# Packed keys of six batches: from two PE transpose steps to one PE step and one crossbar transfer

## The chip, the cores and the metric

The kernel runs on one core of one Trainium2 chip. The metric is the device time of one execution in microseconds (us); the profile gives a slightly shorter span, from the first to the last instruction. The core has five engines that run side by side: PE (matmul), DVE (VectorE), ACT (ScalarE), POOL (GpSimd) and SP (here only an issuer of transfers). In the views PEld is PE's loading of weights, and a q behind an engine's name marks an issue of a transfer. A *crossbar transfer* is a DMA that transposes on its way (`dma_start_transpose`). An execution is called slow when it takes over 1.5% more than the fastest of the same kernel.

## The reference, cut to what matters

```python
# batch 8, heads 8, seq 576, head_dim 64, n_pack 32; p is (8, 8, 32, 64)
p_packed = sm_attn(p, k, v)            # p attends to k, v: 32 rows a head
out      = sm_attn(q, p_packed, p_packed)
x = out.transpose(0, 2, 1, 3).reshape(B * S, H * D)
h = x @ w_in                           # 512 -> 2048
g = h * np.cos(h)
result = g @ w_out                     # 2048 -> 512
```

The rows of `p` are the "packed keys" of the title. Their scores against `k` need `p` with the head dimension on the partitions, so `p` has to be transposed once per batch. It is a small job: 8 x 32 rows of 64 per batch.

## The kernel before

For each batch a *slot* of 16 column blocks runs on PE: each block is an h step (four matmuls, L256, called h0 to h15 below), most of them followed by one to three output matmuls (L309) of the batch before as filling. PSUM is divided into `psA`, three buffers of two banks, and `ot`, two of one bank. Every h step, every transpose step in this slot, every pp and every score takes the next `psA` buffer in turn.

```python
A = ctx.enter_context(tc.tile_pool(name="psA", bufs=3, space=PSUM))
O = ctx.enter_context(tc.tile_pool(name="psO", bufs=2, space=PSUM))
...
def xbar(n, b):                         # q or k of batch b through the crossbar
    t = xT[n, b] = att_pool.tile(...)
    nc.sync.dma_start_transpose(out=t, in_=bf[n, b].rearrange("p h x -> p (h x)"))
...
def pack_p(b0, b1, flat=None):          # keys of batches b0..b1-1 on PE
    ng = 2 * (b1 - b0)
    if flat is None:
        flat = psa(BF16).rearrange("p a x -> p (a x)")     # one psA buffer
    for g in range(ng):
        nc.tensor.transpose(flat[:, g * 128:(g + 1) * 128],
                            p_bf[:, 2 * b0 + g].rearrange("p t d -> p (t d)"), ident)
    V.tensor_copy(out=P2[:, b0:b1]..., in_=flat[:, 0:ng * 128])
...
def h_mm(b, fc):
    ps = psa()
    ...                                 # four matmuls into ps
    ACT.activation(out=csv, in_=ps..., func=AF.Sin, bias=PI_HALF)
    def rest():
        V.tensor_tensor(out=gT[b][:, fc, :]..., in0=ps..., in1=csv, op=ALU.mult)
        ...
    return rest
...
slot(1, [..., (7, tk("k", 2, 2)), (9, lambda: pack_p(2, 5)),      # after h9
         (11, lambda: pack_p(5, B)), (12, next_loads)], 4, {3: 3})  # after h11
...                                     # s1(2), pp(2), s2(2), s1(3) ...
xbar("q", 3)
a1_xbar(3)                              # softmax weights of batch 3, crossbar
recips(3)
xbar("k", 4)
...
slot(2, [(7, lambda: pp(3, engs=(ACT, ACT))), (11, lambda: pw2(3))], 5, {11: 3})
```

`pp(b)` multiplies the softmax weights of a batch (a1T) with its permuted v, and so needs both. The loads of v, q and k of the next batches are held on POOL until the transpose of an earlier k has landed.

The softmax here doesn't subtract the row's maximum and nothing guards it: scores larger than these inputs give would overflow.

## Time and profile before

| | before |
|---|---|
| time, median (runs) | 249.25 us (3); 249.08, 249.09, 249.07 and 248.85 in the later comparisons (6, 11, 12, 11) |
| profiled span | 247.0 us |
| PE / DVE / ACT / POOL busy | 95 / 67 / 68 / 23% |
| PE time for the 12 transposes in slot 1 | 0.34 + 0.33 us |
| PE lost in waits of h10 and h13 there | 0.22 + 0.22 us |

The lines behind this table stand in the prediction. The one thing to bring along: with PE at 95% nothing counts that does not free PE or keep it from a wait.

### The profile page before, as it was taken

The numbers are of one execution on the slowest core, as the hardware profiler recorded it, in microseconds if no ns is written. First come the engines' busy times: TensorE is split into PE (matmuls) and PEld (weight loads), VectorE is DVE, ScalarE is ACT, GpSimd is POOL, SyncE is SP. The second block draws the span as 40 slices with busy tenths as digits, with TensorE's granted clock in tenths as the row PEclk, the third lists the DMA queues.
The fourth block names the chain that finished last, engine by engine and source line by source line (L and its number), as shares of the span: only waits on it lengthen the run. The fifth ranks groups of instructions, "written<-read, shape, count | busy, mean of one in ns | idle before, by whom it ended". The sixth has DMA issues, their size and how long they took to land.

```text
span 247.0 us, 5038 instructions
## 1 busy us (share of the span) xinstructions
PE 234.0 (95%) x2004; PEld 131.4 (53%) x2037; DVE 165.9 (67%) x249; ACT 169.0 (68%) x282; POOL 57.7 (23%) x70
## 2 busy tenths in 40 slices
PE   8888799999999999999999999999999999999993
PEld 3454374566545654565446554565456554665452
DVE  3549987678668876678767766678766684886110
ACT  2369799877666887888787776888778684873000
POOL 8342543240500455022404005030500000000000
PEclk9999999999999999999999999999999999999999
DMA  6999999999899999999998986999591113111133
GB/s 86 203 203 206 205 206 229 200 241 165 165 193 167 223 157 217 215 204 161 213 178 170 192 175 83 195 163 184 109 155 26 45 42 85 45 30 55 48 82 85
DMA packets 63175, 37.09 MB, mean 150 GB/s; under 512 B 35792, under 2 KB 58576, under 8 KB 63152
## 3 DMA queue, kind: packets, MB, share of 16 engines
q0 software_dynamic: 23152, 18.75, 49.8%
q1 hardware_dynamic: 39568, 17.83, 34.7%
q10 hardware_dynamic: 432, 0.20, 0.4%
q8 instruction: 16, 0.26, 0.4%
q14 instruction: 7, 0.06, 0.1%
HBM read 37.22 MB, written 9.44 MB: 189 GB/s over the span
## 4 chain that ended last, share of the span: by engine, by line
PE 80%; DMA 10%; DVE 3%; issue 2%; ACT 2%; POOL 2%; DVEq 0%; POOLq 0%
PE ot L309 46%; PE psA L256 22%; DMA vbf<-in_v_dram 10%; PE psA L207 3%; PE psA L129 2%; DVE gT L263 2%; PE psA L183 2%; ACT cosT L260 2%; PE ot L295 1%; PE psA L233 1%; POOL vp L77 1%; ACT ppT L75 1%; POOL kbf L84 1%; PE ot L104 0%; DVE vp L77 0%
## 5 line engine op out<-in xcount | busy, mean ns | idle before, releaser
L309 PE MATMUL ot<-w_out_bf,gT 128*128 128x512 bf16 x481 | 127.0, 379 | 2.2 <-issue 1.4
L263 DVE TENSOR_TENSOR gT<-psA,cosT 128x576 bf16<-128x576 f32 x128 | 93.9, 755 | 28.3 <-ACT cosT L260 27.5
L260 ACT ACTIVATE cosT<-psA 128x576 bf16<-128x576 f32 x128 | 82.4, 652 | 25.1 <-PE psA L256 22.4
L256 PE MATMUL psA<-a2n,PPW 128*128 128x288 bf16 x512 | 83.8, 286 | 1.5 <-DVE PPW L77 0.4
L309 PEld LDWEIGHTS <-gT 128*128 128x128 bf16 x512 | 47.8, 98 | 43.3 <-issue 6.5
L256 PEld LDWEIGHTS <-PPW 128*128 128x128 bf16 x512 | 49.3, 98 | 34.8 <-issue 4.1
L77 DVE CAST PPW<-psA 128x1024 bf16<-128x1024 f32 (+1 forms) x23 | 26.9, 1175 | 11.6 <-PE psA L207 11.5
L267 POOL COPY joint<-gT 128x512 bf16<-128x512 bf16 x16 | 9.8, 615 | 86.1 <-DVE gT L263 86.1
L77 DVE COPY osb<-ot 128x512 f32<-128x512 f32 (+1 forms) x22 | 14.9, 678 | 17.5 <-PE ot L309 7.6
L77 POOL COPY vp<-vbf 96x3072 bf16<-96x3072 bf16 x7 | 19.3, 2751 | 6.5 <-DMA vbf<-in_v_dram 6.5
L75 ACT COPY osb<-ot 128x512 f32<-128x512 f32 (+1 forms) x15 | 8.5, 567 | 15.3 <-PE ot L309 10.6
L243 DVE SCALAR_TENSOR_TENSOR a2n<-a2u,r,lns 128x576 bf16<-128x576 bf16 x16 | 12.3, 812 | 7.3 <-ACT lns L241 7.3
L235 ACT ACTIVATE lns<-psA 128x576 f32<-128x576 f32 x16 | 10.2, 651 | 7.1 <-PE psA L233 6.5
L140 ACT ACTIVATE a<-psA 128x576 bf16<-128x576 f32 x16 | 10.3, 647 | 6.7 <-PE psA L129 6.7
L309 PE MATMUL ot<-w_out_bf,joint 128*128 128x512 bf16 x48 | 13.0, 379 | 0.1
L225 ACT ACTIVATE a2u<-psA,rs 128x576 bf16<-128x576 f32 x16 | 11.0, 737 | 1.4 <-PE psA L129 1.3
L75 ACT CAST ppT<-psA 64x128 bf16<-64x128 f32 x24 | 6.2, 260 | 6.6 <-DVE ppT L77 5.9
L207 PE MATMUL psA<-w_in_bf,ppT 64*32 64x512 bf16 x224 | 10.1, 380 | 0.0
L241 ACT ACTIVATE lns<-lns 128x576 f32<-128x576 f32 x16 | 10.0, 676 | 0.0
L347 PE MATMUL ot<-wz 128*128 128x512 bf16 x23 | 8.2, 491 | 1.4 <-DVE wz L358 1.2
L84 POOL DMA_DIRECT2D vbf<-in_v_dram x8 | 6.2, 775 | 6.2 <-DVE vp L77 4.2
L525 POOL COPY gate<-kT 1x1 bf16<-1x1 bf16 x3 | 0.5, 180 | 30.1 <-DMA kT<-kbf 30.1
(73 smaller groups left out, 154.9 us busy)
## 6 DMA issues: line engine op xcount, KB each, us to landing
kbf<-in_k_dram POOLq DMA_DIRECT2D x8, 576.0 KB, 12.2
vbf<-in_v_dram POOLq DMA_DIRECT2D x8, 576.0 KB, 7.3
qbf<-in_q_dram POOLq DMA_DIRECT2D x8, 576.0 KB, 9.7
out_dram<-osb SPq DMA_DIRECT2D x24, 192.0 KB, 2.6
out_dram<-osb SPq DMA_DIRECT2D x22, 128.0 KB, 2.4
w_in_bf<-in_moe_w_in_dram POOLq DMA_DIRECT2D x4, 512.0 KB, 17.4
w_out_bf<-in_moe_w_out_dram POOLq DMA_DIRECT2D x4, 512.0 KB, 21.1
out_dram<-osb SPq DMA_DIRECT2D x26, 64.0 KB, 2.1
```

Of the source, the lines that this page charges most:

```text
L75: ACT.copy(out=out, in_=in_)
L77: eng.tensor_copy(out=out, in_=in_)
L140: ACT.activation(out=a1[b % 2][:, y, :, 0:TP].rearrange("p (e m) x -> p e m x", e=2), in_=ps[y][:, :, 0:HS].rearrange("p e (m x) -> p e m ...
L207: nc.tensor.matmul(ps[y][32 * x:32 * x + 32, :], ppT[b % 2][r, 2 * x + y, :], w_in_bf[r, x, n * 512:(n + 1) * 512], start=True, stop=True)
L225: ACT.activation(out=a2u[b][:, y].rearrange("p (e x) -> p e x", e=2), in_=ps[y][:, :, 0:HS], func=AF.Exp, scale=rs1[b][:, y:y + 1])
L235: ACT.activation(out=lns[b][:, y].rearrange("p (e x) -> p e x", e=2), in_=ps[:, :, 0:HS], func=AF.Ln)
L241: ACT.activation(out=lns[b][:, y], in_=lns[b][:, y], func=AF.Exp, scale=-1.0)
L243: V.scalar_tensor_tensor(out=a2n[b][:, y], in0=a2u[b][:, y], scalar=r1[b][:, y:y + 1], in1=lns[b][:, y], op0=ALU.mult, op1=ALU.mult)
L256: nc.tensor.matmul(ps[:, e, 0:HS], PPW[b][:, y, fc * 128:(fc + 1) * 128], a2n[b][:, y, e * HS:(e + 1) * HS], start=(y == 0), stop=(y == 1))
L260: ACT.activation(out=csv, in_=ps[:, :, 0:HS], func=AF.Sin, bias=PI_HALF)
L263: V.tensor_tensor(out=gT[b][:, fc, :].rearrange("p (e x) -> p e x", e=2), in0=ps[:, :, 0:HS], in1=csv, op=ALU.mult)
L309: nc.tensor.matmul(pss[c], w, w_out_bf[:, fc, :], start=(fc == 0), stop=(fc == NFC - 1))
```

## The change

The intent is to take packed-key transposes off PE. The keys of batches 4 to 7 are not needed for another 40 us, so a crossbar transfer can bring them; those of batches 2 and 3 stay on PE, in one step.

```diff
     slot(1, [..., (5, tk("k", 2, 0)), (6, tk("k", 2, 1)),
-             (7, tk("k", 2, 2)), (9, lambda: pack_p(2, 5)),
-             (11, lambda: pack_p(5, B)), (12, next_loads)], 4, {3: 3})
+             (7, tk("k", 2, 2)), (9, lambda: pack_p(2, 4)), (12, next_loads)], 4, {3: 3})
@@
     xbar("k", 4)
+    nc.sync.dma_start_transpose(
+        out=P2[:, 4:B].rearrange("p b (g h) n -> p (b g) (h n)", g=2),
+        in_=p_bf[:, 8:2 * B].rearrange("p g t d -> p (g t d)"))
     fill(5)
```

## The prediction

> **What bounds the kernel now.** I began with the busy times on the page, because they say which engine a saving must land on, and then the shares of the chain that ended last.
>
> ```profile
> PE 234.0 (95%) x2004; PEld 131.4 (53%) x2037; DVE 165.9 (67%) x249; ACT 169.0 (68%) x282; POOL 57.7 (23%) x70
> ...
> PE 80%; DMA 10%; DVE 3%; issue 2%; ACT 2%; POOL 2%; DVEq 0%; POOLq 0%
> ```
>
> PE is busy for 95% of the 247.0 us span, with the clock at full speed in every slice. It carries 80% of the chain, and the DMA share of that chain (10%) is all before 29 us, the start-up loads. So an operation taken off PE after 29 us is worth its PE time, and a wait on PE is worth its length. Time on DVE or in the DMA queue is worth nothing unless it makes PE wait. Next I read what the key transposes cost, from the instructions on the packed keys.
>
> ```profile
> L117 PE MATMUL psA<-ident,p_bf x14: 219/219/311, 4.2 to 58.5; 128*128 128x128 bf16 x14
> ```
>
> 219 ns is the latency of one, not what it takes from PE, so I looked at PE's own timeline around the two steps that the change touches (start, length, what).
>
> ```profile
> 55.84 0.50 PE L117 MATMUL psA<-ident,p_bf 128*128 128x128 bf16 x6
> 56.18 0.59 PE L309 MATMUL ot<-w_out_bf,gT 128*128 128x512 bf16 x2
> 56.83 0.65 PE L256 MATMUL psA<-a2n,PPW 128*128 128x288 bf16 x4
> 57.31 0.59 PE L309 MATMUL ot<-w_out_bf,gT 128*128 128x512 bf16 x2
> 57.75 0.65 PE L256 MATMUL psA<-a2n,PPW 128*128 128x288 bf16 x4
> 58.24 0.50 PE L117 MATMUL psA<-ident,p_bf 128*128 128x128 bf16 x6
> 58.57 0.59 PE L309 MATMUL ot<-w_out_bf,gT 128*128 128x512 bf16 x2
> 59.01 0.65 PE L256 MATMUL psA<-a2n,PPW 128*128 128x288 bf16 x4
> 59.49 0.38 PE L309 MATMUL ot<-w_out_bf,gT 128*128 128x512 bf16 x1
> 59.93 0.65 PE L256 MATMUL psA<-a2n,PPW 128*128 128x288 bf16 x4
> ```
>
> Starts give the throughput. Six transposes take 56.18 - 55.84 = 0.34 us, the second time 0.33, thus 56 ns each. Four h matmuls (L256) take 0.49 us, and one output matmul (L309) takes 0.43/2 = 0.215. There are two holes. After 56.18 the two output matmuls are through at 56.61 and the next h starts at 56.83 (0.22 lost). After 59.49 the one is through at 59.71 and the next h starts at 59.93 (0.22 lost again). The chain in order of time says what ends both:
>
> ```profile
> 56.02 0.77 DVE gT L263
> 56.79 0.04 issue
> 56.83 0.65 PE psA L256 x4
> ...
> 59.12 0.77 DVE gT L263
> 59.89 0.04 issue
> 59.93 0.65 PE psA L256 x4
> ```
>
> psA has three buffers, given in turn to h of each column block and to each key transpose step. An h buffer is free only when DVE has multiplied by the cosine. With a key step in the turn, h10 needs the buffer of h8, and h13 that of h11: only two h are in flight, and PE catches up.
>
> **What the Trainium skill says.** "TensorE: Matmul & The Clock Gate", Part 4 (PE-mode transpose): the result lands in PSUM and needs a copy out; it gives about 275 to 390 ns for one of 128x128. The need of a copy agrees (line 119 on DVE, 0.55 us for 768 columns); the duration does not, 219 ns here. The same page, "Wait — 56ns, not 53.3ns?", gives 55.6 ns from start to start at full clock with 128 columns; the 56 ns above agrees, and it is the figure that counts. "Perfetto Trace Analysis", Optimization Strategy: a bubble that repeats can mean too few PSUM buffers; the two 0.22 us holes agree. "DMA: Bandwidth & Descriptors", Rules for kernel authors: crossbar transposes from different queues must be serialized, one beside ordinary transfers needs nothing. All of this kernel's are issued by SP, the new one too; the trace before shows them running beside stores and loads.
>
> **The change part by part.** *Removed:* 8 of 12 transposes in this stretch. The instruction order of the changed kernel has four left after h9 and none after h11; the DVE copies of 768 and 768 columns become one of 512; everything else is in the same order. By throughput that is 8 x 56 = 0.45 us of PE. What arrives has to be walked, because of the holes.
>
> First step (after h9): two fewer transposes would have PE ready 0.11 us earlier, but h10 still waits for h8's multiply to end at 56.79. Gain 0, the hole grows from 0.22 to 0.33. The step still takes a buffer.
>
> Second step (after h11): it goes altogether. h12 follows two output matmuls: 58.24 + 0.43 = 58.67 in place of 59.01, a gain of 0.34. Its buffer is then that of the first key copy, free at about 57.40 + 0.42 (DVE copies: 0.29 us for 256 columns, 0.55 for 768). h13 now needs h10's buffer, which is free at 58.20 + 0.76 = 58.96, before PE gets there at 58.67 + 0.49 + 0.22 = 59.38. The 0.22 hole closes, and the gain is 0.55. h14 needs h11's multiply (ends at 59.88) and comes at 59.38 + 0.49 + 0.43 = 60.30; h15 needs h12's (cosine done about 59.99, multiply about 60.77) and comes at 61.22 against 61.77. So 0.34 + 0.22 = about 0.55 us of PE, more than the 0.45 of the transposes because a buffer wait goes with them. The last cosine is earlier too, so the table load and the first exponentials of batch 2 keep pace.
>
> *Added:* one crossbar transfer of 128 x 1024 bf16, 256 KB, on SP behind that of k4. Of SP's timeline:
>
> ```profile
> 78.50 3.16 SPq L156 DMA_TRANSPOSE a1T<-a  x1
> 81.76 3.04 SPq L93 DMA_TRANSPOSE kT<-kbf  x1
> 84.89 12.19 SPq L316 DMA_DIRECT2D out_dram<-osb  x8
> ```
>
> a1T has 12 blocks of 128 columns; its undisturbed issues take 1.44 to 1.59 us and it lands in 4.0. The new one has 8 blocks: by estimate 8/12 x 1.5 = 1.0 us of SP's time, landing about 1.0 + (4.0 - 1.5) = 3.5 us after 84.9, near 88.4. Its first reader, the scores of batch 4, loads weights at 97.99, so it is some 9 us early. It holds the stores back by about 1 us; they feed nothing soon (four output buffers, and the next two copies come at 89.35 and 95.25).
>
> *Carried to the end?* PE then reaches every later point 0.55 us sooner, while some feeders keep DMA time. Batch 3's pp is the closest:
>
> ```profile
> 80.88 2.75 POOL L77 COPY vp<-vbf 96x3072 bf16<-96x3072 bf16 x1 [2.07 <-DMA vbf<-in_v_dram]
> ...
> 84.43 0.93 PEld L183 LDWEIGHTS <-vp 96*128 96x128 bf16 x24
> ```
>
> v is permuted at 83.63, and a1T lands at 78.50 + 5.2 = 83.7 (its slowest landing). PE would ask at 84.43 - 0.55 = 83.88. That passes with 0.2 to 0.3 us to spare. Sum: 249.25 - 0.55 = 248.70 us.
>
> **The rivals.** *A wait at batch 3's pp takes some of it back.* The slack is only 0.2, and 0.2 us of jitter in the loads would cost 0.1 to 0.2 us: 248.8 to 248.9. *The new transfer delays the loads of v4, q4 and k5.* They wait for k4's transpose to land at 86.7, are issued from 87.67, and q4 lands about 98.5, just before its own transpose at 98.64; then comes a1T of batch 4 (102.43 + 4.0 = 106.4), which pp reads at 108.4. The new bytes come behind k4's in the same queue, and the transfer view shows the engines nearly idle from about 88.8 to 90.2 before the loads start. 262 KB at the 288 GB/s that k4's transpose reached is 0.9 us, which fits. A delay would have to exceed 2.0 - 0.55 = 1.4 us to reach PE. If it did, the gain is gone: 249.2 to 250. *The transposes hide anyway.* Were the stretch paced wholly by ACT and DVE, the gain would be nil. It speaks for this that the first step's saving does vanish in a hole; against it, that PE starts h10 to h12 back to back. Then 249.2. *DVE as the bound* I rule out: it is at 67%, and its copies shrink.
>
> **Range and chances.** The three runs before lie within 0.33 us, so the gain is hardly larger than their spread. The low end takes 0.55 plus a better drop of waits and a low run, the high end a load delay that eats the gain: 248.2 to 249.4. Two per cent is 5 us, ten times anything in the sum: faster by over 2% 0.01, within 0.98, slower 0.01 (a stall of every later stage by displaced loads).
>
> **What would show it.** Right: 8 fewer transposes; h12 some 0.92 us after h11 in place of 1.26, no hole before h13, one still before h10 (about 0.33); batch 2's first scores about 0.55 us sooner than 63.65; the new transfer issued near 84.9 in about 1 us, landed by 89; PE's start at batch 4's scores near 97.4; no new wait at pp of batches 3 and 4. Wrong: a hole before h13, a PE wait for v or a1T at 84 or 108, loads issued later than 88, or a time under 248.2 or over 249.4.

## The result, and the profile after

The changed kernel took 248.31 us (median of 6, 248.00 to 248.62) beside 249.08 (248.73 to 249.37) for the kernel before. The ratio is 0.9971, 95% interval 0.9958 to 0.9984: 0.72 us less, between 0.40 and 1.05.

First the page of the changed kernel: busy time, and the chain that ended last by engine and by line.

```profile
PE 233.2 (94%) x1996; PEld 130.9 (53%) x2029; DVE 165.2 (67%) x248; ACT 169.0 (68%) x282; POOL 57.7 (23%) x70
...
PE 78%; DMA 12%; issue 2%; DVE 2%; ACT 2%; POOL 2%; DVEq 0%; POOLq 0%
PE ot L309 46%; PE psA L256 21%; DMA vbf<-in_v_dram 10%; PE psA L207 3%; DMA a1T<-a 2%; PE psA L129 2%; PE psA L183 2%; DVE gT L263 2%; PE ot L295 1%; PE psA L233 1%; ACT cosT L260 1%; POOL vp L77 1%; ACT ppT L75 1%; POOL kbf L84 1%; PE ot L104 0%
```

Eight matmuls and one DVE copy fewer, as the edit says. But DMA has grown from 10% to 12% of the chain, and the new part has a name: a1T, a crossbar transfer on which PE waited.

Next PE's timeline in the stretch of the change (start, length, what, and in brackets the idle time before it and its releaser). It answers to the ten lines of before in the prediction; h9 starts at 55.25 here and 55.35 there.

```profile
55.74 0.39 PE L117 MATMUL psA<-ident,p_bf 128*128 128x128 bf16 x4
55.96 0.59 PE L309 MATMUL ot<-w_out_bf,gT 128*128 128x512 bf16 x2
56.72 0.65 PE L256 MATMUL psA<-a2n,PPW 128*128 128x288 bf16 x4 [0.17 <-DVE gT L263]
57.21 0.59 PE L309 MATMUL ot<-w_out_bf,gT 128*128 128x512 bf16 x2
57.64 0.65 PE L256 MATMUL psA<-a2n,PPW 128*128 128x288 bf16 x4
58.13 0.59 PE L309 MATMUL ot<-w_out_bf,gT 128*128 128x512 bf16 x2
58.56 0.65 PE L256 MATMUL psA<-a2n,PPW 128*128 128x288 bf16 x4
59.05 0.38 PE L309 MATMUL ot<-w_out_bf,gT 128*128 128x512 bf16 x1
59.27 0.65 PE L256 MATMUL psA<-a2n,PPW 128*128 128x288 bf16 x4
```

The hole before h10 is still there and has grown: 55.96 + 0.43 = 56.39, and h10 starts at 56.72 (0.33; the bracket says 0.17 because it counts from the modelled end of the matmul before). h12 follows h11 by 0.92 in place of 1.26. Between h12 and h13 there is nothing to wait for: 58.56 + 0.49 + 0.22 = 59.27. h15 starts 5.86 us after h9 (61.11 - 55.25); before it was 6.42.

What PE then gains is lost in part at batch 3's pp, on PE's timeline of the changed kernel:

```profile
84.43 0.86 PE L183 MATMUL psA<-a1T,vp 96*128 96x64 bf16 x24 [0.38 <-DMA a1T<-a]
```

a1T was issued at 78.92 and took 5.4 us to land. So this one profiled execution ends only 0.2 us before the one of the kernel before (246.8 against 247.0), though it was 0.65 ahead at 72 us. To compare executions fairly I cut each profile at three marks: the start of h9 in slot 1 (all before it is the same code in both kernels), the start of batch 2's sums (L233), and the end of the last matmul.

| profile | start-up: to h9 | stretch: h9 to sums | rest: sums to end |
|---|---|---|---|
| before | 55.35 | 17.62 | 170.04 |
| changed | 55.25 | 17.07 | 170.50 |

The stretch gained 0.55 us. The rest lost 0.46 at pp (0.38 waiting, and the weights of v, which came with the wait, loaded late). The marks are these lines, of before and of the changed kernel (the window asked for cuts the group after three of its four matmuls; only the start counts here):

```profile
72.97 0.53 PE L233 MATMUL psA<-a2u,ones_blk 128*128 128x288 bf16 x3
```

```profile
72.32 0.53 PE L233 MATMUL psA<-a2u,ones_blk 128*128 128x288 bf16 x3
```

The new transfer on SP's timeline of the changed kernel:

```profile
78.92 2.43 SPq L156 DMA_TRANSPOSE a1T<-a  x1
81.44 3.87 SPq L93 DMA_TRANSPOSE kT<-kbf  x1
85.40 1.26 SPq L487 DMA_TRANSPOSE P<-p_bf  x1
```

It took 1.26 us to issue and 3.2 us to land, at 88.6. Its reader came at 97.81.

### The profile page after: what moved, and what is told of

It is laid out like the page before. It is cut to its first block, busy times and chain, and to the rows that moved or that the text cites. A ratio compares the mean times of both kernels' runs of the same rounds, so it can differ in the third digit from the quotient of the medians.

```text
span 246.8 us, 5023 instructions
## 1 busy us (share of the span) xinstructions
PE 233.2 (94%) x1996; PEld 130.9 (53%) x2029; DVE 165.2 (67%) x248; ACT 169.0 (68%) x282; POOL 57.7 (23%) x70
## 4 chain that ended last, share of the span: by engine, by line
PE 78%; DMA 12%; issue 2%; DVE 2%; ACT 2%; POOL 2%; DVEq 0%; POOLq 0%
PE ot L309 46%; PE psA L256 21%; DMA vbf<-in_v_dram 10%; PE psA L207 3%; DMA a1T<-a 2%; PE psA L129 2%; PE psA L183 2%; DVE gT L263 2%; PE ot L295 1%; PE psA L233 1%; ACT cosT L260 1%; POOL vp L77 1%; ACT ppT L75 1%; POOL kbf L84 1%; PE ot L104 0%
## 5 line engine op out<-in xcount | busy, mean ns | idle before, releaser
L77 POOL COPY vp<-vbf 96x3072 bf16<-96x3072 bf16 x7 | 19.3, 2751 | 6.3 <-DMA vbf<-in_v_dram 6.3
L183 PEld LDWEIGHTS <-vp 96*128 96x128 bf16 x192 | 6.5, 98 | 2.3 <-issue 1.2
```

Source lines behind the costliest of these rows:

```text
L77: eng.tensor_copy(out=out, in_=in_)
L183: nc.tensor.matmul(ps[:, hp * 64:(hp + 1) * 64], vp[b][:, c, hp * 128:(hp + 1) * 128], a1T[b][0:TP, :, j, 32 * hp:32 * hp + 32], start=(j ...
```

## The experiments

**Theory**: the gain is a *buffer turn*. A PE transpose step between h steps takes one of three psA buffers, and PE then waits for DVE. The second step's turn is gone, and that brings the 0.55 us. **Rival 1**: the gain is the PE time of the eight transposes, 56 ns each. **Rival 2**: the added transfer costs something in the loads behind it. **Rival 3**: the wait for a1T at pp is regular, and the true gain of the stretch is hidden by it.

All eleven runs gave the right result. The first eight ran on one chip, in two groups of four, the last three on another. Each time is beside the kernel before on the same chip; r5 to r8 are compared with the eleven times of it that r1 to r4 have, plus one more. The times scatter by 0.3 us and more, so for questions of 0.1 us the three marks decide, and the times only have to agree. Each mark comes from a single profile of its kernel. The start-up is what scatters: it took 55.25 to 57.01 us in these profiles, in the same code (only r7 and r8 issue their transfer before this mark). The 57.01 (r6) has a stretch of low clock in it (0.50 to 0.55 from 31 to 34 us). r7, r8 and r11 each had one slow run; the ratios leave it out, the ranges below include it.

| profile | start-up | stretch | rest | ratio to before (95%) |
|---|---|---|---|---|
| before | 55.35 | 17.62 | 170.04 | |
| changed | 55.25 | 17.07 | 170.50 | 0.9971 (0.9958 to 0.9984) |
| r1 changed again | 55.74 | 17.07 | 170.03 | 0.9969 (0.9946 to 0.9992) |
| r2 one PE step of 12 | 55.54 | 17.19 | 170.03 | 0.9975 (0.9951 to 0.9998) |
| r3 two PE steps of 2, transfer | 55.61 | 17.63 | 170.03 | 0.9983 (0.9958 to 1.0009) |
| r4 before, transfer added | 56.02 | 17.62 | 170.04 | 0.9996 (0.9968 to 1.0024) |
| r5 changed, pp later | 55.61 | 17.07 | 170.17 | 0.9975 (0.9948 to 1.0001) |
| r6 before, pp later | 57.01 | 17.63 | 170.17 | 1.0006 (0.9978 to 1.0034) |
| r7 all keys by crossbar | 55.66 | 16.51 | 174.39 | 1.0078 (1.0036 to 1.0120) |
| r8 the same, pp later | 55.35 | 16.51 | 171.25 | 1.0022 (0.9980 to 1.0064) |
| r9 PE step after h14 | 55.59 | 16.86 | 170.36 | 0.9985 (0.9972 to 0.9998) |
| r10 the same, pp later | 55.30 | 16.86 | 170.01 | 0.9964 (0.9952 to 0.9976) |
| r11 transfer ahead of k4 | 55.36 | 17.08 | 173.58 | 1.0023 (0.9988 to 1.0059) |

### r1: the changed kernel again

No edit.

> The changed kernel once more, unaltered, to have it on the same chip as the next three. Theory (buffer turn: the whole gain comes from the second key step no longer taking one of the three psA buffers): 0.55 us below the kernel before, ratio about 0.998. If batch 3's a1T lands later than PE wants it, as in the first profile, 0.2 to 0.4 us of that goes again in that execution. Rival (the first result's 0.72 us is real and something beyond the stretch gained): ratio 0.997 again.

248.53 us (248.34 to 248.80) beside 249.09. The stretch is 17.07 again, and this time PE did not wait at pp, which came at the same time:

```profile
84.46 0.86 PE L183 MATMUL psA<-a1T,vp 96*128 96x64 bf16 x24
```

Two things differ. In the first profile q3's transpose, which a1T's follows on SP, had been issued at 73.08; here at 72.08, and in the kernel before at 71.99. It waits for q3's load. Of that 1 us only 0.2 reaches a1T, which is issued at 78.71 in place of 78.92 and takes 5.4 us to land both times. The larger part is PE: its start-up took 55.74 in place of 55.25, so it is ready for a1T 0.5 us later. r11 below, whose code is that of the changed kernel up to this pp, started h9 at 55.36 and waited 0.15 us here. So the wait at pp is a matter of how PE and the loads of one execution stand to each other, and it comes when PE is early. The rest takes 170.03 without it, as before.

### r2: one PE step of 12 transposes, no transfer

```diff
-             (7, tk("k", 2, 2)), (9, lambda: pack_p(2, 5)),
-             (11, lambda: pack_p(5, B)), (12, next_loads)], 4, {3: 3})
+             (7, tk("k", 2, 2)), (9, lambda: pack_p(2, B)),
+             (12, next_loads)], 4, {3: 3})
```

> The kernel before with all 12 key transposes of batches 2 to 7 in one PE step after h9, copied at once (1536 columns); no crossbar transfer. PE does as many transposes as before; only the second buffer turn is gone. Buffer-turn theory: the first step now takes 0.67 us of PE and h10 starts about 0.1 us later than before, but h12 and h13 come sooner, in all 0.4 to 0.5 us gained (ratio 0.998). Rival (the gain is the PE time of the transposes, 56 ns each): nothing removed, so no gain, ratio 1.000.

248.59 us (248.43 to 248.93) beside 249.09. PE does every transpose that it did before, and the stretch is still 0.43 us shorter. PE's timeline of this kernel:

```profile
56.03 0.83 PE L117 MATMUL psA<-ident,p_bf 128*128 128x128 bf16 x12
56.70 0.59 PE L309 MATMUL ot<-w_out_bf,gT 128*128 128x512 bf16 x2
57.13 0.65 PE L256 MATMUL psA<-a2n,PPW 128*128 128x288 bf16 x4
```

12 transposes take 0.67 us, and h10 comes at once: 56.70 + 0.43 = 57.13. The six more transposes fill the hole in which PE waited for h8's buffer anyway. Rival 1 expected no gain here. Most of the change's gain thus needs no transfer at all.

### r3: the change, with its four PE transposes in two steps

```diff
-             (7, tk("k", 2, 2)), (9, lambda: pack_p(2, 4)), (12, next_loads)], 4, {3: 3})
+             (7, tk("k", 2, 2)), (9, lambda: pack_p(2, 3)), (11, lambda: pack_p(3, 4)), (12, next_loads)], 4, {3: 3})
```

> The changed kernel with its four PE transposes split into two steps of two, after h9 and after h11, where the kernel before has them; the crossbar transfer stays. PE does 8 transposes fewer than before, as in the change, but both buffer turns are there. Buffer-turn theory: h10 and h13 wait as before, no gain, ratio 1.000 (within 0.1 us). Rival (transposes' PE time): as the changed kernel, 0.45 us or more gained, ratio 0.998.

248.93 us (248.66 to 249.18) beside 249.09: unclear by time (the interval includes 1), but the stretch is 17.63, the length before to 0.01 us. Eight transposes fewer, and nothing gained. PE's timeline:

```profile
58.50 0.28 PE L117 MATMUL psA<-ident,p_bf 128*128 128x128 bf16 x2
58.61 0.59 PE L309 MATMUL ot<-w_out_bf,gT 128*128 128x512 bf16 x2
59.27 0.65 PE L256 MATMUL psA<-a2n,PPW 128*128 128x288 bf16 x4
59.76 0.38 PE L309 MATMUL ot<-w_out_bf,gT 128*128 128x512 bf16 x1
60.19 0.65 PE L256 MATMUL psA<-a2n,PPW 128*128 128x288 bf16 x4
```

PE is ready for h12 at 58.61 + 0.43 = 59.04 and starts it at 59.27; ready for h13 at 59.76 + 0.22 = 59.98 and starts it at 60.19. Each transpose taken away came back as waiting. With r2 this settles it between the theory and rival 1: at these places the number of steps decides, the number of transposes hardly.

### r4: the kernel before with the transfer added

```diff
     xbar("k", 4)
+    nc.sync.dma_start_transpose(out=P2[:, 4:B]..., in_=p_bf[:, 8:2 * B]...)   # same values once more
     fill(5)
```

> The kernel before with both PE steps kept and the crossbar transfer added behind k4's, writing the same values over the same keys. It costs what the transfer costs and saves nothing. Theory: about 1.0 to 1.3 us of SP, stores later by that, nothing on PE: ratio 1.000, no new PE wait. Rival (the transfer delays the loads of v4, q4, k5 and so a1T of batch 4): 0.2 us or more slower and a PE wait for a1T near 108 us.

249.07 us (248.65 to 250.29) beside 249.09, the stretch 17.62 and the rest 170.04: no PE wait. The transfer is not free in the queue, though. v4's load, issued when k4 has landed, takes 7.0 to 7.6 us to land in the profiles with this transfer (changed, r1, r3, r4, r5) and 6.3 to 6.4 without it (before, r2, r6). From the issue of that load to the issue of batch 4's a1T it is 15.06 to 16.16 us with it and 14.76 to 15.01 without, 0.5 us more in the mean. The later profiles blur this: with the transfer r9 took 8.5 us for v4's load and 15.87 to a1T, r10 7.5 and 14.88; and r8, with no transfer at this place, took 7.8 us for the load. In r1 a1T then lands at 107.6 and PE asks at 108.19; in r2, without the transfer, it is 106.6 and 108.10. So what these single profiles show for rival 2 is a delay of about half a microsecond in the mean, with ranges that overlap, and slack takes it. The least slack that was left is 0.4 us, in r9 (a1T at 107.8, PE at 108.15).

### r5 and r6: batch 3's pp two blocks later, in the changed kernel and in the one before

```diff
-    slot(2, [(7, lambda: pp(3, engs=(ACT, ACT))), (11, lambda: pw2(3))], 5, {11: 3})
+    slot(2, [(9, lambda: pp(3, engs=(ACT, ACT))), (11, lambda: pw2(3))], 5, {11: 3})
```

> The changed kernel with batch 3's pp moved from after h7 to after h9 of that stretch, so that it comes some 1.8 us later than PE asked for a1T. In the first profile PE waited 0.38 us there for a1T by DMA. If that wait is regular: 0.3 to 0.4 us faster than the changed kernel, ratio to before about 0.9965. If it is a matter of when the loads land in one execution and mostly absent: like the changed kernel, 0.9975 to 0.998. In either case no PE wait for a1T near 84 us in the profile.

> Control for the run before it: the kernel before with the same move of batch 3's pp and nothing else. It had no wait there in its profile, so both theories expect 1.000 within 0.1 us; a gain here would say that moving pp is worth something of its own.

248.57 us (248.36 to 249.17) and 249.25 (248.96 to 250.61), both beside 249.07. No wait for a1T in r5, and no gain over r1 that the times show; their intervals are too wide to tell 0.4 us. What makes rival 3 fall is r1's profile: with pp in its old place PE does not wait there, so the wait is not regular. The move costs 0.13 to 0.14 us in both (rest 170.17), which I had not expected for the control; pp takes a psA turn too, and where it stands has its price.

### r7 and r8: all six batches by one crossbar transfer

```diff
+    def xbar_p():                       # 12 blocks, batches 2 to 7
+        nc.sync.dma_start_transpose(out=P2[:, 2:B]..., in_=p_bf[:, 4:2 * B]...)
@@
-    slot(1, [..., (4, lambda: (xbar("q", 2), xbar("k", 3))), ..., (9, lambda: pack_p(2, 4)), (12, next_loads)], 4, {3: 3})
+    slot(1, [..., (4, lambda: (xbar_p(), xbar("q", 2), xbar("k", 3))), ..., (12, next_loads)], 4, {3: 3})
```

The later transfer of the change is dropped; r8 also has pp at 9.

> The change carried further: no key step on PE for batches 2 to 7; one crossbar transfer of 128 x 1536, issued before q2's and k3's, in a stretch where SP has nothing to do (about 49 to 55 us). Buffer-turn theory: h10's wait (0.33 us in the changed kernel) goes, and 0.22 us of transposes: 1.1 us below before at the end of the stretch, 0.5 to 0.6 below the changed kernel there; then PE comes to batch 3's pp at about 83.3 us, before v and a1T (83.7 to 84.3), and waits 0.3 to 1.0 us. Ratio 0.996 to 0.998. Rival: the transfer pushes q2, k3 and the loads behind them, and the gain is lost: 1.000.

> The run before with batch 3's pp two column blocks later, so that the DMA chain of batch 3 no longer meets PE. Theory: the whole 1.1 us reaches the end, ratio about 0.9955. Rival (another feeder by DMA takes the place): no better than the run before.

251.45 us (249.90 to 253.77) and 249.75 (248.49 to 252.94), beside 249.07. One run of each was slow (253.77 and 252.94). The stretch did what the theory said, 1.11 us shorter. But the transfer runs into the loads of v2, q2 and k3. The issue list of r7 shows it:

```profile
P<-p_bf SPq DMA_TRANSPOSE x1, 13.1
```

It takes 13.1 us to land, against 3.2 for two thirds of the bytes in the changed kernel. q2's load takes 19.3 us to land in place of 16.2 (15.4 to 17.4 in all profiles without this transfer), q2's transpose is issued at 58.38 in place of 55.57, everything behind it moves, and PE waits 2.59 us for batch 3's a1T. It gets worse after the wait. These are PE's line of r7, and the row of one stretch (busy time by engine, then the granted clock, DMA share and GB/s):

```profile
86.50 0.86 PE L183 MATMUL psA<-a1T,vp 96*128 96x64 bf16 x24 [2.59 <-DMA a1T<-a]
```

```profile
88.00:91.00 3.00, 3.00 (x14) 1.59 (x12) 0.76 (x1) 1.52 (x4) 0.75 (x2) 0.56 0.91 204
```

In the 3 us after the wait the granted clock is 0.56 (its mean over the kernel before is 1.000), and from pp to the next slot's scores PE takes 12.18 us in place of 10.52. So a wait of 2.6 us costs 4.3: 170.04 + 2.68 (pp later than its place, counted from the sums) + 1.66 = 174.38. The times show it too: the three runs of r7 with a mean clock of 0.993 took 252.28 to 253.77, the three at 1.000 took 249.90 to 250.62. In r8 pp waits 0.80 us, the clock stays at 1.00, and the rest is 1.21 longer: 0.80 for the wait, 0.13 for the moved pp, and 0.28 more, of which 0.20 goes just before batch 4's pp (at 108.46, its a1T landed at 108.3). r7 was expected at 0.996 to 0.998 and r8 at 0.9955: the theory's hope that the gain reaches the end failed in both; rival "pushes the loads" holds.

### r9 and r10: the PE step where it costs least

```diff
-             (7, tk("k", 2, 2)), (9, lambda: pack_p(2, 4)), (12, next_loads)], 4, {3: 3})
+             (7, tk("k", 2, 2)), (12, next_loads), (14, lambda: pack_p(2, 4))], 4, {3: 3})
```

r10 has pp at 8 as well (the edit of r5 with an 8).

> The changed kernel with its remaining PE key step moved from after h9 to after h14, where the column blocks before and after it are each followed by two output matmuls. Walk with the buffer-turn theory: after h9 no step, so h10 comes at once (0.56 us before the changed kernel's predecessor had it); the step then costs its 0.22 us and a wait of about 0.06 for h13's multiply. From h9 to the sums of batch 2: 0.83 us less than the kernel before (17.62 us from h9's start), against 0.55 less in the changed kernel. In the whole: 0.3 us below the changed kernel if batch 3's a1T does not meet it, ratio 0.9965; the same as it, with a PE wait near 84 us, if it does. Rival (a step costs the same wherever it stands): 0.55 less, as the changed kernel.

> The run before with batch 3's pp one column block later (after h8), to take a1T's landing off PE's way: no PE wait for a1T by DMA near 84 us; the move itself may cost up to 0.14 us, as moving it by two blocks did. Ratio 0.9965 to 0.997; the fastest version if the run before waits.

248.54 us (248.15 to 248.82) and 247.99 (247.88 to 248.18), both beside 248.85. The stretch is 0.76 us shorter than before, 0.21 better than in the changed kernel with the same transposes and the same transfer, so a step does not cost the same wherever it stands. The walk had said 0.83; PE's timeline has the difference:

```profile
59.99 0.65 PE L256 MATMUL psA<-a2n,PPW 128*128 128x288 bf16 x4
60.54 0.38 PE L117 MATMUL psA<-ident,p_bf 128*128 128x128 bf16 x4
```

The step itself waits 0.06 us for a buffer (59.99 + 0.49 = 60.48), which I had left out. In r9's profile pp waits 0.23 us for a1T and 0.32 is lost there; in r10 there is no wait, and the move to this place costs nothing (170.01). r10 is the fastest kernel here: 0.9964 to before, its five times do not overlap with any of its before, and on the same chip it is 0.55 us (median) under r9. Against the changed kernel, run on other chips, it is ahead by its stretch (0.21 us); by time that is not separated, as the intervals overlap.

### r11: the transfer ahead of k4

```diff
-    xbar("k", 4)
     nc.sync.dma_start_transpose(out=P2[:, 4:B]..., in_=p_bf[:, 8:2 * B]...)
+    xbar("k", 4)
```

> The changed kernel with the crossbar transfer issued ahead of k4's transpose, not behind it. k4's transpose then starts about 1.3 us later, and with it the loads of v4, q4, k5 and a1T of batch 4. Theory (the place behind k4 matters, as a1T of batch 4 lands only 0.85 us ahead of PE in the changed kernel's profile): a PE wait for a1T of 0.2 to 1.0 us near 108 us, ratio 0.998 to 1.001. Rival (the transfer is hidden wherever it stands): like the changed kernel, 0.9975, no wait near 108.

249.15 us (248.36 to 253.01) beside 248.85; the ratio of 1.0023 is unclear, as its interval includes 1. k4's transpose is issued at 83.26 in place of 81.44, q4's at 101.15 in place of 99.58, and a1T of batch 4 comes late. PE's line at pp of batch 4, and the row after it:

```profile
109.92 0.86 PE L183 MATMUL psA<-a1T,vp 96*128 96x64 bf16 x24 [1.77 <-DMA a1T<-a]
```

```profile
110.00:113.00 3.00, 3.00 (x34) 1.98 (x34) 0.28 (x1) 1.69 (x5) 0.00 (x0) 0.64 0.91 200
```

The wait is 1.77 us, more than the 0.2 to 1.0 that I expected, and again the clock falls, to 0.64, which costs 1.43 more up to the next scores. Of the six times the two with a mean clock of 0.993 are 251.74 (the profiled one) and 253.01 (a slow run); the other four lie between 248.36 and 249.19. So it seems that in some executions the slack still holds and in some it does not. "Behind k4's" in the change is thus no detail: ahead of it, the transfer can cost several times what the change gains.

## Why the prediction was right, point by point

- **Time.** 248.70 us was predicted, a gain of 0.55; measured were 248.31 and 0.72 (0.40 to 1.05), in r1 0.77 (0.20 to 1.35), in r5 0.62 (-0.02 to 1.30). Right in range and in sign; 248.31 lies 0.39 under the figure predicted and 0.11 above the low end. The part that belongs to the edit is 0.55 by the profiles (17.62 to 17.07, three times). Whether the surplus of some 0.2 us is more than scatter of the start-up stays open.
- **First step: gain 0, the hole grows to 0.33.** Exactly so. r2 shows the other side of it: eight transposes more in that hole cost the stretch 0.12 us against the changed kernel, not 0.45.
- **Second step: 0.34 and the hole before h13 closed.** h12 after 0.92 us, no wait at h13. The sum of 0.55 stands.
- **"More than the transposes because a buffer wait goes with them."** Right, and too modest. r2 gains 0.43 with all transposes in place and r3 gains nothing with eight gone. The step, not its transposes, was the cost.
- **The added transfer.** 1.0 us of SP was estimated, 1.26 measured; landing at 88.4, measured 88.6. The SP time taken in proportion to blocks was a fifth too small.
- **"262 KB at 288 GB/s is 0.9 us, which fits."** What this was to show, that the loads behind are not delayed, failed, without harm. The stores went out 1.9 us later (86.76 for 84.89), of which the transfer took 1.36. v4's load took 7.1 us to land in place of 6.3, and batch 4's a1T landed at 107.3 in place of 106.4. That stayed under the 1.4 us of slack that I had worked out, so it did not reach PE. r11 shows what happens when it does. The loads were issued at 88.25, past the 88 that I had named as a sign of being wrong. k4's transpose, which gates them, was issued at 81.44, even 0.32 before its time in the kernel before, but took 5.7 us to land in place of 4.9. With the new transfer right behind it, it took 5.2 to 6.0 us in all seven profiles, against 4.9 in before, r2 and r6; since r8 took 5.8 with nothing new behind it, the transfer is not shown to be the cause.
- **Batch 3's pp.** The slack of 0.2 to 0.3 us was the right worry, and a PE wait at 84 was the second sign of being wrong that came true. a1T landed at 84.3, not 83.7. The slack was gone in one of two profiles of the changed kernel (and in r11's, with a wait of 0.15), and there the loss was 0.46 us, where the rival had allowed 0.1 to 0.2. How many of the six timed executions waited is not known, so that the time came out in range in spite of it owes something to luck. Batch 4's scores then came at 97.81, not 97.4.
- **"219 ns is the latency of one", and so not the skill's 275 to 390.** The ends of matmuls are modelled in these profiles, so 219 ns is no measurement of it. The sum does not use it; the 56 ns come from starts, and they hold.

## What to carry to other kernels

Where PE work goes through a small ring of PSUM buffers, an extra step costs its turn in the ring more than its matmuls: walk the ring buffer by buffer, and first try to join two steps into one or to put the step where the blocks around it are long. A transfer that "nobody needs for 10 us" still stands in a queue: look at what is issued behind it, and keep it behind the transfer that gates the next loads. When a kernel's executions differ by more than the effect, cut the profiles at marks around the edit and compare the pieces.

## What the Trainium skill lacked or had wrong

- "TensorE: Matmul & The Clock Gate", Part 4 (PE-mode transpose) gives 275 to 390 ns for one 128x128 transpose. It lacks what a row of them takes: here they start 56 ns apart. (The profiles have 219 ns for one, but with a modelled end, so they don't show the page wrong.) In this kernel even the 56 ns say little: 12 in place of 4 made the stretch 0.12 us longer (r2 against the changed kernel).
- The same page, "Why this matters for your kernels", warns of PE gaps of more than about 3 us between bursts. Here waits of 1.77 us (r11) and 2.59 us (r7) were each followed by 3 us at a granted clock of 0.64 and 0.56, and cost 1.43 and 1.66 us on top; a wait of 0.80 us (r8) left the clock at 1.00. Length alone does not decide: in the start-up of r6 a wait of 1.23 us for w_in was followed by a clock of 0.50 to 0.55 from 31 to 34 us, while waits of 1.27 to 1.32 us at the same place (r1, r2, r4) left it at 1.00. What else decides was not tested.
- "DMA: Bandwidth & Descriptors", Rules for kernel authors, says that a transpose next to ordinary transfers needs nothing. All eleven results were right, so for correctness the runs agree; for time that rule gives no cost. The 384 KB transpose issued among three loads took 13.1 us to land, against 3.2 us for 256 KB in a quieter stretch, and q2's load took 19.3 us in place of 15.4 to 17.4.
- No page gives what SP spends on issuing a crossbar transpose of this kind on this chip; sequencer times stand only in a part on trn3, as its "before" figures and for other sizes. Here 8 blocks of 128 columns took 1.26 to 1.65 us and 12 blocks 1.44 to 1.59 when undisturbed.
